# Attention units that alternate between two sets of PSUM banks, in a list-scheduled attention, mixing and FFN kernel

## The chip, the core and the metric

The kernel runs on one core of a Trainium2 chip. Its engines work side by side: TensorE (PE, and PEld for its weight loads) multiplies, VectorE (DVE) and ScalarE (ACT) work element by element, GpSimd (POOL) takes small element-wise work and some transfers, SyncE (SP) starts most transfers. Products land in PSUM, eight banks of 512 fp32 values on each of 128 partitions. The metric is the device time of one execution in microseconds (us).

## What is computed

Windowed attention over 8 batches and 8 heads, then a Fourier mixing over sequence and channels, a normalisation, and an FFN. Cut to what matters:

```python
# q, k, v: (8, 8, 576, 64); heads 0-3 look at 32 neighbours, heads 4-7 at 32 rows with stride 4
scores = np.where(masks, scale * q @ k.T, -1e9)
attn = exp(scores - max) / (sum + 1e-9);  x = attn @ v          # then (8, 576, 512)
mixed = np.real(np.fft.fft(np.fft.fft(x, axis=1), axis=2))
u = x + mixed
un = (u - mean) / sqrt(var + 1e-6)
out = u + np.maximum(un @ w_ch1, 0) @ w_ch2                     # 512 -> 2048 -> 512
```

## The kernel before

All work is written down as operations with an engine, an estimated cost, a priority and the buffers they use. A planner (class `Plan`) then runs a list schedule: whenever an engine is free in the plan, the ready operation with the lowest priority number that finds its buffers free is put next. The result is a fixed order of instructions on each engine. On the chip each engine follows its order and waits by semaphores.

Attention (`attend`) is cut into 96 units, 12 for each batch. A unit makes the scores of two blocks of 96 queries for two heads (4 products, L557), adds the mask and takes the negated maximum (4 DVE operations, L566), takes exponentials (4 ACT operations, L572), transposes (4 on PE, L585), copies the result to SBUF (ACT, L588), multiplies by the values (4 products, L592, called the AV products here) and divides by the sums (three DVE operations, L600, L603, L604). PE's profile rows show two matmuls for each product at L557 and L592.

Mixing of a batch (`mix`: products at L774, L796, L820, L826) follows its attention. Weights come in as 64-bit words and are narrowed on ACT and DVE (`narrow`). A fill (`fill`) runs the first 6 of 16 slices of the FFN for 256 tokens while attention of later batches goes on: up products at L954, down products at L970. After attention the rest of the FFN runs (L1223, L1311, L1278).

The eight PSUM banks are shared out by name: `pair` (banks 0 and 1) for scores, bank 2 for transposes (`pt`), bank 3 for AV products (`av`), banks 4 and 5 for mixing (`mixes`), banks 6 and 7 for the fills (`zs`). A ring of a tag hands its slots out in turn; `behind` says that a tag's first slot may be taken only when another tag's buffers are all done with. The scores of a unit use 256 columns of both banks of `pair`, one unit the lower half, the next the upper half. The AV products of each unit use bank 3.

Until the first fill takes its bank, the planner fills PE's free time with pairs of products on a blank tile (L503, called spins here; up to 250 pairs). They keep PE active and compute nothing that is used. They stand in PE's order like any other instruction.

The priority numbers (`P_...`) set the order of attention, mixing, weight loads, stores and fills against each other.

Of the kernel before, what the change touches and what calls it, by code (L numbers as in the profile page):

```python
# [36 lines left out]
NPE = 1  # L37
LO1 = 'DVE'
NFA = 5
P_QK0, P_V0 = -8.0, -7.0  # L40
P_ST, P_FD, P_WD, P_ST0, P_FD0, P_SPAN0, P_SPAN1 = -4.0, -12.0, -10.0, -14.0, -14.0, 4.0, 13.0
P_QK, P_V, P_TR, P_MIX, P_SPAN, P_W, P_WF, P_FILL, P_FILLT = -8.0, -7.0, -5.0, 2.0, 13.0, 24.0, 4.0, 45.0, 4.0
P_MIX0, P_MIX1 = -14.0, 0.0
T_SEQ, T_CHN = 20.0, 27.0
NCH = B * S // TOK
NREST = 4 * B
# [130 lines left out]
    __slots__ = ("eng", "cost", "fn", "prio", "bufs", "after", "waits", "ready", "start", "num", "nbytes")  # L177


PSUM_TAGS = ("sc", "half", "pt", "av", "mix", "ff", "duo0", "duo1", "duo2")  # L180


class Plan:
# [200 lines left out]
def fused_kernel(ctx: ExitStack, tc, q, k, v, w1, w2, seq, tail, chn, alt, mask, ident, perm, flip, out):  # L384
    nc = tc.nc
    plan = Plan()
# [21 lines left out]
    pair, pt_av, mixes, zs = [eight[i:i + 2] for i in range(0, 8, 2)]  # L408
    views = {"sc": pair, "pt": pt_av[:1], "av": pt_av[1:], "mix": mixes, "ff": zs}
    views.update({f"duo{i}": [lambda i=i: eight[2 * i:2 * i + 2]] for i in range(3)})  # L410
    plan.behind.update({"sc": ("half",), "duo0": ("sc", "half"), "duo1": ("pt", "av"), "duo2": ("mix",)})

    def halves():
        b = Buf(None, "half")
        plan.slots["half"] = 2
        line = plan.tags.setdefault("half", [])
        lo = 256 * (len(line) % 2)
        b.make = lambda: [t[:, lo:lo + 256] for t in pair]
        line.append(b)
        return b  # L420

    def ring(tag, of):
        b = Buf(None, tag)
        plan.slots[tag] = len(of)
        line = plan.tags.setdefault(tag, [])
        ap = of[len(line) % len(of)]
        b.make = ap if callable(ap) else lambda: ap
        line.append(b)
        return b

    def bank(tag):
        return ring(tag, views[tag])
# [53 lines left out]
    def start():  # L486
        dma(lambda: nc.sync.dma_start(out=mask_sb(), in_=mask), (), (mask_sb,), -7.9, QB * 3 * KB * 4)
        dma(lambda: nc.sync.dma_start(out=ident_sb(), in_=ident), (), (ident_sb,), -7.8, P * 3 * P * 4)
        dma(lambda: nc.sync.dma_start(out=perm_sb(), in_=perm), (), (perm_sb,), -7, QB * QB * 12)
        dma(lambda: nc.sync.dma_start(out=flip_sb(), in_=flip), (), (flip_sb,), 50, P * 32)  # L490

        def zero(t, eng, cost, fn, key=None, prio=-5.0):
            add(eng, cost, fn, (), ((t, key) if key is not None else t,), prio)

        zero(half, "DVE", 0.07, lambda: nc.vector.memset(half(), -0.5))
        for n, t in enumerate(kbs):
            zero(t, "DVE", 0.1, lambda t=t: nc.vector.memset(t()[:, 0:WIN], 0.0), "z", -6.0 + n)
        zero(blank, "DVE", 0.3, lambda: nc.vector.memset(blank().bitcast(F32), 0.0), None, -9.0)
        spin = Buf(ap=zs[0])
        for n in range(NSPIN):  # L500
            def turn_over():
                for _ in range(2):
                    nc.tensor.matmul(spin()[:, :2 * P], lhsT=blank()[:, :P], rhs=blank()[:, P:3 * P], start=True, stop=True)  # L503
            add("PE", 0.22, turn_over, (blank,), (spin,), SPIN, at=0.4 * n)
        for t in xs + xtail:
            zero(t, "DVE", 0.07, lambda t=t: nc.vector.memset(t()[:, C:C + 1], 0.0), "pad")
        def gaps():
            for r in (32, 96):
                nc.vector.memset(eot().bitcast(F32)[r:r + 32, 0], 0.0)
        zero(eot, "DVE", 0.4, gaps, ("gap", 0))  # L510
        zero(eot, "DVE", 0.2, lambda: nc.vector.memset(eot().bitcast(F32)[0:32, 1], 0.0), ("gap", 1))
        zero(ye, "DVE", 0.2, lambda: nc.vector.memset(ye().bitcast(F32), 0.0))
        for b in range(B):
            dma(lambda b=b: nc.sync.dma_start(
                out=xsm[b]()[0:1], in_=blank()[0:1].bitcast(F32),
            ), (blank,), ((xsm[b], "zero"),), 12 * b + 6, 2048)
        for i in range(2):
            for m in range(2):
                add("POOL", 0.06, lambda i=i, m=m: nc.gpsimd.dma_start(out=seq_sb[i]()[:, m], in_=seq[i, m]),
                    (), ((seq_sb[i], m),), 6 + i, P * 2 * NSP * 4, at=T_SEQ + i)  # L520
                add("POOL", 0.06, lambda i=i, m=m: nc.gpsimd.dma_start(out=chn_sb[i]()[:, m], in_=chn[i, m]),
                    (), ((chn_sb[i], m),), 9 + i, P * 2 * NEP * 4, at=T_CHN + i)
        add("POOL", 0.06, lambda: nc.gpsimd.dma_start(out=tail_sb(), in_=tail), (), (tail_sb,), 6.5, P * 3 * NSP * 4, at=T_SEQ + 0.5)
        add("POOL", 0.06, lambda: nc.gpsimd.dma_start(out=alt_sb(), in_=alt), (), (alt_sb,), 8, P * NEP * 4, at=T_SEQ + 4)
# [23 lines left out]
    def attend(b, dil, j, u, tq, kb, vt, xt, prio):  # L548
        blocks = (u, u + 3) if dil else (2 * u, 2 * u + 1)
        masks = DIL_MASK if dil else PLAIN_MASK  # L550
        sc = halves()

        def scores():
            for n, t in enumerate(blocks):
                for e in range(2):
                    ps = slice(64 * e, 64 * e + 64)
                    nc.tensor.matmul(  # L557
                        sc()[e][:QB, KB * n:KB * n + KB], lhsT=tq()[ps, QB * t:QB * t + QB],
                        rhs=kb()[ps, QB * t:QB * t + KB], start=True, stop=True,
                    )  # L560
        add("PE", 0.62, scores, (tq, kb), (sc,), prio)
        pm = attw("pm", [QB, 4, KB], F32, 3)
        mx = attw("mx", [QB, 4], F32, 3)
        for i in range(4):
            def masked(i=i):
                nc.vector.tensor_tensor_reduce(  # L566
                    pm()[:, i], sc()[i % 2][:QB, KB * (i // 2):KB * (i // 2) + KB], mask_sb()[:, masks[blocks[i // 2]]],
                    -0.125, 3.0e38, ALU.add, ALU.min, mx()[:, i:i + 1],
                )
            add("DVE", 0.21, masked, (sc, mask_sb), ((pm, i), (mx, i)), prio)  # L570
        for i in range(4):
            add("ACT", 0.295, lambda i=i: nc.scalar.activation(  # L572
                out=pm()[:, i], in_=pm()[:, i], func=AF.Exp, bias=mx()[:, i:i + 1], scale=-1.0),
                ((mx, i),), ((pm, i),), prio)
        ps = bank("pt")
        for i in range(4):
            def turn(i=i):
                t = blocks[i // 2]
                if dil:
                    order = perm_sb()[:, t % 3]  # L580
                elif t < 3:
                    order = ident_sb()[:QB, 0, :QB]
                else:
                    order = ident_sb()[:QB, 1, P - QB:]
                nc.tensor.transpose(ps()[:, QB * i:QB * i + QB], pm()[:, i], order)  # L585
            add("PE", 0.087, turn, ((pm, i), perm_sb, ident_sb), ((ps, i),), prio)
        pt = attw("ptsb", [P, 4, QB], F32, 3)
        add("ACT", act(4 * QB) - 0.05, lambda: nc.scalar.copy(  # L588
            out=pt().rearrange("p i q -> p (i q)"), in_=ps()[:, :4 * QB]), (ps,), (pt,), prio)
        av = bank("av")  # L590
        for i in range(4):
            add("PE", 0.173, lambda i=i: nc.tensor.matmul(  # L592
                av()[:QB, 65 * i:65 * i + 65], lhsT=pt()[:, i],
                rhs=vt()[:, i % 2, blocks[i // 2]], start=True, stop=True),
                (pt, vt), ((av, i),), prio)
        sums, rinv = attw("sums", [QB, 4], F32, 3), attw("rinv", [QB, 4], F32, 3)

        def view():
            return av()[:QB, :260].rearrange("p (t h d) -> p t h d", t=2, h=2)
        add("DVE", 0.075, lambda: nc.vector.tensor_scalar(  # L600
            sums(), av()[:QB, :260].rearrange("p (i d) -> p i d", d=65)[:, :, D], 1e-9, None, op0=ALU.add),
            (av,), (sums,), prio)
        add("DVE", 0.1, lambda: nc.vector.reciprocal(out=rinv(), in_=sums()), (sums,), (rinv,), prio)  # L603
        add("DVE", dve(256), lambda: nc.vector.tensor_tensor(  # L604
            out=xt()[:, :, j::2, :], in0=view()[:, :, :, 0:D],
            in1=rinv().rearrange("p (t h) -> p t h", t=2).unsqueeze(3).broadcast_to([QB, 2, 2, D]), op=ALU.mult),
            (av, rinv), ((xt, j),), prio)
        if j == 1:
            store(b, dil, u, xt, prio)
# [792 lines left out]
```

## Time and profile before

| | |
|---|---|
| median of 3 runs | 1089.67 us (1085.24 to 1094.61) |
| the profiled execution's own time | 1086.16 us |
| its span in the trace | 1084.4 us |
| PE busy | 1067.1 us (98%) |
| DVE busy | 775.9 us (72%) |
| ACT busy | 517.7 us (48%) |
| spins on PE | 248 matmuls, all in the first 108 us |

The span runs from the first to the last instruction of the program; 1.76 us of the execution's time lie outside it. Ends of matmuls are modelled, so PE's busy time covers small stalls between matmuls. A matmul's cost in a row of them is read from start to start, which the chain of waits gives.

### The profile page before, as it was taken

The numbers are of one execution on the slowest core, as the hardware profiler recorded it, in microseconds if no ns is written. First come the engines' busy times: TensorE is split into PE (matmuls) and PEld (weight loads), VectorE is DVE, ScalarE is ACT, GpSimd is POOL, SyncE is SP. The second block draws the span as 40 slices with busy tenths as digits, with TensorE's granted clock in tenths as the row PEclk, the third lists the DMA queues.
The fourth block names the chain that finished last, engine by engine and source line by source line (L and its number), as shares of the span: only waits on it lengthen the run. The fifth ranks groups of instructions, "written<-read, shape, count | busy, mean of one in ns | idle before, by whom it ended". The sixth has DMA issues, their size and how long they took to land.

```text
span 1084.4 us, 21164 instructions
## 1 busy us (share of the span) xinstructions
PE 1067.1 (98%) x7683; PEld 958.8 (88%) x7683; DVE 775.9 (72%) x2384; ACT 517.7 (48%) x1282; POOL 280.7 (26%) x328
## 2 busy tenths in 40 slices
PE   7999999999999999999999999999999999999998
PEld 6888888898889888889989898999898999888987
DVE  4889988777677757976774657676766767676746
ACT  5777656547456553434342543434342525252532
POOL 2236463644343326553321110101010101010200
PEclk9999999999999999999999999999999999999999
DMA  9686566745464326254443402223233332333221
GB/s 342 223 269 196 165 167 180 235 134 176 121 210 140 115 64 176 78 163 127 148 137 98 117 20 59 98 60 98 60 104 74 96 81 88 88 82 91 67 71 39
DMA packets 103800, 137.10 MB, mean 126 GB/s; under 512 B 9144, under 2 KB 61816, under 8 KB 103696
## 3 DMA queue, kind: packets, MB, share of 16 engines
q1 hardware_dynamic: 100128, 126.85, 39.9%
q0 software_dynamic: 3040, 8.09, 2.5%
q8 instruction: 60, 0.98, 0.4%
q10 hardware_dynamic: 528, 0.82, 0.2%
q14 instruction: 44, 0.36, 0.1%
HBM read 97.92 MB, written 37.80 MB: 125 GB/s over the span
## 4 chain that ended last, share of the span: by engine, by line
PE 89%; DVE 5%; DMA 3%; issue 1%; ACT 1%; POOL 0%; SPq 0%; DVEq 0%; ACTq 0%
PE bank L1223 23%; PE bank L1311 19%; PE bank L970 12%; PE bank L954 12%; PE bank L592 5%; PE bank L557 5%; PE bank L820 3%; PE bank L585 3%; PE bank L774 2%; PE bank L503 2%; PE bank L1278 1%; DMA ut<-in_w_dram 1%; DMA vt<-in_v_dram 1%; DVE pm L566 1%; DMA wst<-in_w_dram 1%
## 5 line engine op out<-in xcount | busy, mean ns | idle before, releaser
L1223 PE MATMUL bank<-low,wb 128*128 128x512 f32 x1080 | 260.4, 393 | 0.0
L1223 PEld LDWEIGHTS bank<-low,wb 128*128 128x128 f32 x1080 | 198.4, 188 | 41.0
L954 PE MATMUL bank<-ut,low 128*128 128x256 f32 x1296 | 175.3, 286 | 1.2 <-DVE low L962 0.8
L954 PEld LDWEIGHTS bank<-ut,low 128*128 128x128 f32 x1296 | 160.9, 189 | 5.2 <-DVE low L962 1.9
L572 ACT ACTIVATE pm<-pm,mx 96x128 f32<-96x128 f32 x384 | 131.2, 394 | 53.8 <-DVE mx L566 49.6
L970 PE MATMUL bank<-low 128*128 128x512 f32 x648 | 155.2, 392 | 0.9 <-DVE low L962 0.9
L998 POOL DMA_INDIRECT ut<-us,flip_sb x20 | 40.3, 2014 | 406.9 <-DVE ut L1055 249.5
L970 PEld LDWEIGHTS bank<-low 128*128 128x128 f32 x648 | 119.1, 188 | 24.7 <-DVE low L962 1.1
L1229 ACT ACTIVATE xa<-bank 128x256 f32<-128x256 f32 x90 | 34.4, 382 | 180.0 <-PE bank L1223 180.0
L566 DVE CUSTOM_DVE_ANT_0 pm<-bank,mask_sb 96x128 f32<-96x128 f32 x384 | 93.0, 278 | 34.5 <-PE bank L557 31.6
L1250 DVE TENSOR_TENSOR y<-xa 128x384 f32<-128x384 f32 x45 | 25.1, 557 | 106.6 <-ACT xa L1229 106.3
L592 PE MATMUL bank<-vt,ptsb 128*96 128x65 f32 x768 | 82.2, 247 | 3.0 <-DVE xt L604 2.5
L592 PEld LDWEIGHTS bank<-vt,ptsb 128*96 128x96 f32 x768 | 76.4, 164 | 9.3 <-DVE xt L604 5.3
L1077 DVE STREAM_TRANSPOSE ut<-ut 128x512 f32<-128x512 f32 (+1 forms) x76 | 71.5, 983 | 18.1 <-DMA ut<-us 17.1
L962 DVE SCALAR_TENSOR_TENSOR low<-bank,low 128x256 fp32r<-128x256 f32 x108 | 45.2, 419 | 47.8 <-ACT low L960 47.1
L960 ACT ACTIVATE low<-bank 128x256 fp32r<-128x256 f32 x108 | 41.3, 382 | 78.1 <-PE bank L954 78.0
L1311 PEld LDWEIGHTS bank<-w2s,low 128*128 128x128 f32 x588 | 73.8, 190 | 2.4
L1044 DVE TENSOR_TENSOR ut<-ut,bank 128x512 f32<-128x512 f32 (+1 forms) x136 | 73.1, 547 | 2.3
L1311 PE MATMUL bank<-w2s,low 128*128 128x256 f32 x588 | 74.4, 281 | 0.0
L557 PE MATMUL bank<-kb,tq 64*96 64x128 f32 x768 | 63.2, 285 | 4.4 <-DVE mx L566 2.3
L1311 PEld LDWEIGHTS bank<-w2s,hm 128*128 128x128 f32 x483 | 59.7, 189 | 1.9
L1311 PE MATMUL bank<-w2s,hm 128*128 128x256 f32 x483 | 60.2, 280 | 0.0
(147 smaller groups left out, 1808.3 us busy)
## 6 DMA issues: line engine op xcount, KB each, us to landing
vt<-in_v_dram SPq DMA_DIRECT2D x32, 390.0 KB
us<-uc SPq DMA_DIRECT2D x36, 257.0 KB
tq<-in_q_dram SPq DMA_DIRECT2D x32, 288.0 KB
part<-row SPq DMA_DIRECT2D x36, 256.0 KB
wst<-in_w_dram SPq DMA_DIRECT2D x18, 512.0 KB
ut<-us SPq DMA_DIRECT2D x36, 256.0 KB
ut<-part SPq DMA_DIRECT2D x36, 256.0 KB
kb<-in_k_dram SPq DMA_DIRECT2D x31, 288.0 KB
```

The costliest lines, as they stand in the source:

```text
L557: nc.tensor.matmul(sc()[e][:QB, KB * n:KB * n + KB], lhsT=tq()[ps, QB * t:QB * t + QB], rhs=kb()[ps, QB * t:QB * t + KB], start=True, stop ...
L566: nc.vector.tensor_tensor_reduce(pm()[:, i], sc()[i % 2][:QB, KB * (i // 2):KB * (i // 2) + KB], mask_sb()[:, masks[blocks[i // 2]]], -0.1 ...
L572: add("ACT", 0.295, lambda i=i: nc.scalar.activation(out=pm()[:, i], in_=pm()[:, i], func=AF.Exp, bias=mx()[:, i:i + 1], scale=-1.0), ((mx ...
L592: add("PE", 0.173, lambda i=i: nc.tensor.matmul(av()[:QB, 65 * i:65 * i + 65], lhsT=pt()[:, i], rhs=vt()[:, i % 2, blocks[i // 2]], start= ...
L954: nc.tensor.matmul(z()[:, :n_tok], lhsT=wf()[:, a, kk], rhs=ut()[:, p, kk], start=(kk == 0 and n == 0), stop=(kk == KT - 1 and n == 2),)
L960: add("ACT", act(n_tok) - 0.05, lambda: nc.scalar.activation(out=h()[:, 0, :n_tok], in_=z()[:, :n_tok], func=AF.Relu), (z,), ((h, 0),), prio)
L962: add("DVE", dve(n_tok), lambda: nc.vector.scalar_tensor_tensor(h()[:, 1, :n_tok], z()[:, :n_tok], 0.0, h()[:, 0, :n_tok].bitcast(F32), op ...
L970: nc.tensor.matmul(acc(), lhsT=h()[:, a, P * s:P * s + P], rhs=wf()[:, p], start=(first and n == 0), stop=(last and n == 2),)
L1044: add("DVE", dve(C if at in (outer, inner) else TOK1), lambda: nc.vector.tensor_tensor(out=blocks(part())[:, at], in0=blocks(part())[:, at ...
L1077: nc.vector.transpose(out=o[back], in_=x[:, g])
L1223: nc.tensor.matmul(z(), lhsT=wb1[NF1 + 2 * p + f]()[:, a, kk], rhs=ut()[:, x, kk], start=(kk == 0 and n == 0), stop=(kk == KT - 1 and n == 2),
L1311: nc.tensor.matmul(acc()[block // 2][:, TOK1 * (block % 2):TOK1 * (block % 2) + TOK1], lhsT=hl()[:, a, i], rhs=w2s[p]()[:, j, x], start=(o ...
```

## The change

Scores of the first 20 units get a ring of two bank sets, the lower halves of banks 0 and 1 and those of banks 4 and 5, which belong to mixing. AV products of the first 29 units alternate between bank 3 and bank 6, which belongs to the fills. Mixing may take its banks only after the 20 units, a fill only after the 29. The spins move from bank 6 to bank 7. Twelve priority numbers are changed (the diff shows one line of them).

```diff
+NSC2, NAV2 = 20, 29
 P_QK0, P_V0 = -8.0, -7.0
-P_ST, P_FD, P_WD, P_ST0, P_FD0, P_SPAN0, P_SPAN1 = -4.0, -12.0, -10.0, -14.0, -14.0, 4.0, 13.0
+P_ST, P_FD, P_WD, P_ST0, P_FD0, P_SPAN0, P_SPAN1 = -5.1, -11.2, -10.0, -19.4, -13.9, 7.8, 13.0
...
-PSUM_TAGS = ("sc", "half", "pt", "av", "mix", "ff", "duo0", "duo1", "duo2")
+PSUM_TAGS = ("sc", "half", "half2", "av2", "pt", "av", "mix", "ff", "duo0", "duo1", "duo2")
...
     views.update({f"duo{i}": [lambda i=i: eight[2 * i:2 * i + 2]] for i in range(3)})
+    views["av2"] = [pt_av[1], zs[0]]
+    plan.behind.update({"av": ("av2",), "ff": ("av2",), "half": ("half2",), "mix": ("half2",)})
     plan.behind.update({"sc": ("half",), "duo0": ("sc", "half"), "duo1": ("pt", "av"), "duo2": ("mix",)})
 
-    def halves():
+    def halves(n):
+        if n < NSC2:
+            return ring("half2", [lambda: [t[:, 0:256] for t in pair], lambda: [t[:, 0:256] for t in mixes]])
         b = Buf(None, "half")
...
-        spin = Buf(ap=zs[0])
+        spin = Buf(ap=zs[1])
...
-        sc = halves()
+        sc = halves(12 * b + 6 * dil + 3 * j + u)
...
-        av = bank("av")
+        av = bank("av2" if 12 * b + 6 * dil + 3 * j + u < NAV2 else "av")
```

In the lists below bankN is PSUM bank N; a line of the changed kernel is 5 higher than the same line before. "waits" names the engine or queue that a row's semaphores belong to.

DVE, the masks of the second unit of the first batch (`pm_247` is its tile of masked scores), before:

```order
L566 ISA pm_247,mx_248<-bank0_135,mask_sb_145 96x128
L566 ISA mx_248 96x1
L566 ISA pm_247,mx_248<-bank1_136,mask_sb_145 96x128
L566 ISA mx_248 96x1
L566 ISA pm_247,mx_248<-bank0_135,mask_sb_145 96x128 [waits PE_49]
```

And now:

```order
L571 ISA pm_247,mx_248<-bank4_139,mask_sb_145 96x128 [waits PE_49]
L571 ISA mx_248 96x1
L571 ISA pm_247,mx_248<-bank5_140,mask_sb_145 96x128 [waits PE_49]
L571 ISA mx_248 96x1
L571 ISA pm_247,mx_248<-bank4_139,mask_sb_145 96x128
```

Before, the second unit's masks waited for PE a second time in the middle of the unit, for scores of the third unit, which PE had been given for the same two banks; now they wait once, for their own scores in banks 4 and 5.

PE, a little later in the first batch, from a spin on: the AV products (`ptsb`), transposes (`pm`) and scores (`kb2`) of three neighbouring units, before:

```order
L503 MATMUL bank6_141<-blank_160 128x256 x2
L585 MATMUL bank2_137<-ident_sb_146,pm_335 128x96 [waits Activation_49]
L592 MATMUL bank3_138<-vt_208,ptsb_401 96x65 [waits DMAHW0_49,DVE_49]
L592 MATMUL bank3_138<-vt_208,ptsb_401 96x65 x3
L585 MATMUL bank2_137<-ident_sb_146,pm_335 128x96 x3
L557 MATMUL bank0_135<-kb2_159,tq_225 96x128 [waits DVE_49]
L557 MATMUL bank1_136<-kb2_159,tq_225 96x128 [waits DVE_49]
```

And now:

```order
L508 MATMUL bank7_142<-blank_160 128x256 x2
L597 MATMUL bank6_141<-vt_208,ptsb_402 96x65 [waits DMAHW0_49,Activation_49]
L597 MATMUL bank6_141<-vt_208,ptsb_402 96x65 x3
L590 MATMUL bank2_137<-ident_sb_146,pm_336 128x96 x4
L562 MATMUL bank0_135<-kb2_159,tq_225 96x128 [waits DVE_49]
L562 MATMUL bank1_136<-kb2_159,tq_225 96x128 [waits DVE_49]
```

The AV products went to bank 6 and no longer wait for DVE, which has the division of the unit ahead to do in bank 3, and they stand ahead of all four transposes.

PE, the stretch ahead of the first fill, with spins between the units' products, before:

```order
L503 MATMUL bank6_141<-blank_160 128x256 x4
L585 MATMUL bank2_137<-ident_sb_146,pm_1505 128x96 [waits Activation_49]
L585 MATMUL bank2_137<-ident_sb_146,pm_1505 128x96 x3
L503 MATMUL bank6_141<-blank_160 128x256 x20
L592 MATMUL bank3_138<-vt_1149,ptsb_1492 96x65 [waits DVE_49]
L592 MATMUL bank3_138<-vt_1149,ptsb_1492 96x65 x3
L557 MATMUL bank0_135<-kb2_159,tq_1281 96x128 [waits DMAHW4_49,DMAHW3_49]
```

And now:

```order
L508 MATMUL bank7_142<-blank_160 128x256 x8
L597 MATMUL bank3_138<-vt_1304,ptsb_1852 96x65 [waits DVE_49]
L597 MATMUL bank3_138<-vt_1304,ptsb_1852 96x65 x3
L508 MATMUL bank7_142<-blank_160 128x256 x8
L590 MATMUL bank2_137<-ident_sb_146,pm_1948 128x96 [waits Activation_49]
L590 MATMUL bank2_137<-ident_sb_146,pm_1948 128x96 x3
L508 MATMUL bank7_142<-blank_160 128x256 x14
L597 MATMUL bank3_138<-vt_1528,ptsb_1931 96x65 [waits DMAHW7_49,DVE_49]
```

Counted over PE's whole order, the first fill stood behind the AV products of 28 units and 248 spins, and now stands behind those of 37 units and 240 spins. Ahead of the AV products of unit 13 there were 122 spins and now are 76; between those of units 29 and 37 there were none and now are 88.

## Rows read from the trace of the kernel before

**Rows 1.** The page's head: busy time, share of the span, instructions.

```profile
span 1084.4 us, 21164 instructions
...
PE 1067.1 (98%) x7683; PEld 958.8 (88%) x7683; DVE 775.9 (72%) x2384; ACT 517.7 (48%) x1282; POOL 280.7 (26%) x328
```

**Rows 2.** Stretches: length, busy time and (instructions) by engine, granted PE clock, DMA.

```profile
8.00:30.00 22.00, 17.32 (x176) 14.31 (x176) 12.97 (x95) 15.39 (x46) 0.54 (x1) 1.00 1.10 386
30.00:78.00 48.00, 47.74 (x470) 43.36 (x468) 40.46 (x206) 36.12 (x99) 14.64 (x14) 1.00 0.72 227
78.00:110.00 32.00, 31.24 (x295) 28.58 (x294) 29.60 (x132) 23.30 (x63) 19.63 (x27) 1.00 0.66 208
...
440.00:1080.00 640.00, 639.62 (x4013) 576.42 (x4010) 438.76 (x819) 257.26 (x568) 97.80 (x76) 1.00 0.32 89
```

**Rows 3.** The spins: durations in ns, first and last start in us.

```profile
L503 PE MATMUL bank<-blank x248: 274/283/579, 1.4 to 108.0; 128*128 128x256 f32 x124
```

**Rows 4.** PE in order of time, to the first fill: start, us, idle before.

```profile
6.87 1.12 PE L557 MATMUL bank<-kb,tq 64*96 64x128 f32 x16
...
16.58 0.68 PE L557 MATMUL bank<-kb,tq 64*96 64x128 f32 x8 [0.57 <-DVE mx L566]
...
24.04 0.89 PE L592 MATMUL bank<-vt,ptsb 128*96 128x65 f32 x8 [0.31 <-DVE xt L604]
...
108.42 2.02 PE L954 MATMUL bank<-ut,low 128*128 128x256 f32 x15
```

**Rows 5.** The chain of waits, pieces in order of time: start, us, what.

```profile
46.34 1.46 PE bank L503 x12
47.80 0.65 PE bank L592 x8
...
48.74 0.61 PE bank L557 x8
...
52.99 0.33 PE bank L585 x4
...
85.49 0.95 PE bank L774 x7
...
89.38 1.45 PE bank L820 x12
```

**Rows 6.** DVE in order of time, one unit's operations: start, us, idle before.

```profile
19.18 0.28 DVE L566 CUSTOM_DVE_ANT_0 pm<-bank,mask_sb 96x128 f32<-96x128 f32 x1
...
19.39 0.28 DVE L566 CUSTOM_DVE_ANT_0 pm<-bank,mask_sb 96x128 f32<-96x128 f32 x1
...
19.82 0.15 DVE L600 TENSOR_SCALAR sums<-bank 96x4 f32<-96x4 f32 x1
20.00 0.17 DVE L603 RECIPROCAL rinv<-sums 96x4 f32<-96x4 f32 x1
20.77 0.29 DVE L566 CUSTOM_DVE_ANT_0 pm<-bank,mask_sb 96x128 f32<-96x128 f32 x1 [0.59 <-PE bank L557]
...
20.98 0.42 DVE L604 TENSOR_TENSOR xt<-bank,rinv 96x256 f32<-96x256 f32 x1
21.32 0.28 DVE L566 CUSTOM_DVE_ANT_0 pm<-bank,mask_sb 96x128 f32<-96x128 f32 x1
```

**Rows 7.** PE's waits (weight loads), 0 to 80 us: us in total, times, longest.

```profile
PEld bank L592 <- DVE xt L604: 1.6, 4, 0.5
...
PEld bank L557 <- DVE xt L604: 1.3, 1, 1.3
PEld bank L557 <- DVE mx L566: 1.3, 3, 0.8
```

**Rows 8.** PE's waits (matmuls) for a transfer, 0 to 80 us.

```profile
PE bank L557 <- DMA tq<-in_q_dram: 2.0, 2, 1.1
```

**Rows 9.** PE's waits (weight loads), 80 to 412 us.

```profile
PEld bank L592 <- DVE xt L604: 3.7, 9, 0.8
PEld bank L557 <- DVE mx L566: 3.4, 9, 0.6
```

More of the change, by code (lines that the diff above doesn't have):

```diff
@@ L39 @@
 NFA = 5
+NSC2, NAV2 = 20, 29
 P_QK0, P_V0 = -8.0, -7.0
-P_ST, P_FD, P_WD, P_ST0, P_FD0, P_SPAN0, P_SPAN1 = -4.0, -12.0, -10.0, -14.0, -14.0, 4.0, 13.0
-P_QK, P_V, P_TR, P_MIX, P_SPAN, P_W, P_WF, P_FILL, P_FILLT = -8.0, -7.0, -5.0, 2.0, 13.0, 24.0, 4.0, 45.0, 4.0
-P_MIX0, P_MIX1 = -14.0, 0.0
+P_ST, P_FD, P_WD, P_ST0, P_FD0, P_SPAN0, P_SPAN1 = -5.1, -11.2, -10.0, -19.4, -13.9, 7.8, 13.0
+P_QK, P_V, P_TR, P_MIX, P_SPAN, P_W, P_WF, P_FILL, P_FILLT = -8.0, -7.7, -5.0, 1.9, 13.0, 24.0, 3.9, 50.3, 4.3
+P_MIX0, P_MIX1 = -16.0, 2.5
 T_SEQ, T_CHN = 20.0, 27.0
```

## The prediction, made before the changed kernel ran

> **What bounds the kernel now.** I read the page's head first. PE is busy for 98% of the span, so little is left between its instructions [rows 1]. The stretches say where that little is: from 440 us to 1080 us PE is busy 639.62 of 640 us, and nothing that happens to attention can shorten it [rows 2]. The end of the program is therefore set by PE's sum of work plus whatever PE loses earlier. It loses in two forms. One is the spins: 248 matmuls without use, the last at 108.0 us [rows 3]. They stand in PE's order and are run whether or not anyone is late. The other is waiting, seen as idle time ahead of scores and AV products [rows 4].
>
> The loss up to the first fill can be added up, because the pieces of the chain of waits give the cost of each kind of product from start to start [rows 5]: a unit's scores 0.61 us, its transposes 0.33, its AV products 0.65, a spin 1.46/12 = 0.122, a mixing product 0.95/7 = 0.136 (L774) or 1.45/12 = 0.121 (the others, and the transposes of normalised rows). By PE's order there stand ahead of the first fill the scores of 35 units (21.4 us), transposes of 32 (10.6), AV products of 28 (18.2), 30 products at L774 and 45 others of mixing (4.1 and 5.4) and 8 more transposes (1.0): 60.6 us in all. Twenty-four spins come before the first score at 6.87 us [rows 4], the other 224 make 27.3 us. The first fill starts at 108.42 us [rows 4], which is 101.55 us after the first score. So 101.55 - 60.6 - 27.3 = 13.7 us were waits and restarts after waits.
>
> What PE waits for there is the unit's own chain. Scores wait for masks of the unit ahead, AV products for the division of the unit ahead [rows 4, 7]; DVE in turn waits 0.59 us for scores in the middle of its run of units [rows 6]. DVE is 59% busy from 8 to 30 us, 84% from 30 to 78 and 92% from 78 to 110 [rows 2].
>
> **Spins.** There are 8 fewer, 8 x 0.122 = **-1.0 us**. This is the only gain that is certain from the order. The 46 spins that go from ahead of unit 13 are not gained: most come back between units 29 and 37, where PE may not start a fill that used to cover it.
>
> **The longer way to the first fill.** By the new order there stand ahead of it the scores of 42 units (25.6 us), transposes of 40 (13.2), AV products of 37 (24.1), the same mixing (9.5) and 16 transposes (1.9): 74.3 us, 13.7 us more than before. It is work that PE would do later anyway, so it costs nothing. With equal waits the first fill would start at 108.42 + 13.7 - 1.0 = 121.1 us. The fills that are pushed back (405 instead of 483 up products ahead of unit 93) move behind attention, where PE has no gaps [rows 2].
>
> **Waits in the first 80 us.** Three of them are what a second set of banks takes away: AV products for the division 1.6 us, scores for the division 1.3, scores for masks 1.3, together 4.2 us [rows 7]. The next thing late is a transfer: scores wait 2.0 us for queries [rows 8], and units that come sooner reach it sooner. Bounds: all 4.2 us go, or nothing goes because every one turns into that wait. I take **-3.5 us**, nearer the first, since only two of the waits before were transfers.
>
> **Waits from 80 us to the first fill.** Units 21 to 29 still have two AV banks. From 80 to 412 us the two kinds of wait are 3.7 and 3.4 us for some 75 units [rows 9], so eight units carry 7.1 x 8/75 = **-0.8 us**. Bounds 0 and 1.5.
>
> **The priorities.** They reorder stores, weight loads and mixing through the rest of attention; no row prices that. The nearest row is the same 7.1 us [rows 9]: it could lose all of it or, at the other end, add as much. With 59 units behind the first fill instead of 68, I take **-1.0 us**, and keep both ends.
>
> **Lent banks.** Mixing has its first product after the scores of 26 units before and of 27 now, past the 20 that hold its banks, so that gate costs 0. If it held mixing longer, a wait would stand in PE's order ahead of L774; none is added. The longest cover for the fills' bank is the spins between units 29 and 37, 88 x 0.122 = 10.7 us, already counted.
>
> **The sum**: -1.0 - 3.5 - 0.8 - 1.0 = -6.3 us on a span of 1084.4, so 1078.1, and 1079.9 for the execution beside 1086.16. The median of the runs stands 3.5 us above the profiled one, so it becomes 1089.67 - 6.3 = **1083.4 us**, 0.6% less.
>
> **Rival 1: DVE becomes what PE waits for, and it is slower.** The new order asks DVE for nine more units ahead of the first fill. A unit costs it 4 x 0.21 + 0.15 + 0.17 + 0.34 = 1.5 us from start to start [rows 6], nine 13.5; one more block of weights less one fill's work I set at 1.5 (estimate, 0 to 3). DVE was busy 83.0 us from 8 to 110 us [rows 2], so about 81.5 to the first fill, 81% of the time. It now has 96.5 us to do. My sum puts the first fill at 121.1 - 4.3 = 116.8 us and so needs DVE at 96.5/108.8 = 89%. At the old 81% the first fill comes at 8 + 119 = 127 us, 6 us of new waits, and the whole is 6 - 1.0 = 5 us **slower: 1094.7 us**. The change is worth nothing at 96.5/114.1 = 85%, and slower by over 1% below 77%. For it speaks that DVE was only 84% busy from 30 to 78 us; against it, that it waited for PE there, which the new banks undo, and that it reached 92% from 78 to 110 us.
>
> **Rival 2: the chain loosens more.** At that 92%, held from 8 us on, DVE would be through at 8 + 105 = 113 us. The waits then shrink by 8 us instead of 4.3, and with spins and later waits the gain is 10 to 11 us: **1079 us**, 1% faster. Against it: the first 30 us move data at 386 GB/s with the queues full [rows 2], which no bank helps.
>
> **Rival 3: the clock.** In all stretches the granted clock was 1.00, the 2.4 GHz level, even from 8 to 30 us where PE idled 4.7 of 22 us [rows 2]. If fewer spins between units 9 and 13 let it fall to 1.2 GHz for those 10 us, products would take twice as long there, some 8 us more: **1091 us**. The Trainium skill ("TensorE: Matmul & The Clock Gate", section "A second HAM failure mode: psum-queue depth-cycling") speaks against a change like this: it tells of a kernel that cycled through PSUM banks and whose small gaps made the clock go up and down. By that rule the sum would turn into this rival; the trace, with larger gaps at 1.00, does not bear it out.
>
> **Chances.** My forecast, 1080.5 to 1088: 0.52. Rival 2 and beyond, 1072 to 1080.5: 0.24. No gain to rival 1, 1088 to 1096: 0.18. Rival 3 or a worse order of the rest: 0.06. The range reaches from 1074 into rival 1, 1094. A measurement of this kernel tells about 1% (11 us) from no change. Faster than 1078.8 is most of rival 2, 0.20; slower than 1100.6 is 0.05; the rest, 0.75, within 1%.
>
> **What would show it.** In the profile after: 240 spins; the first up product of a fill between 114 and 119 us (127 for rival 1, 113 for rival 2); DVE at 89% from 8 us to there; no AV products that wait for the division before unit 29, and fewer mask operations that wait for scores; a clock of 1.00 throughout. I would be wrong if PE's idle time grew between 110 and 440 us, where the new priorities act and I have no price, or if PE lost time behind attention, where more fills now stand.

## The result, and the profile of the changed kernel

The changed kernel takes **1077.51 us** (median of 4 runs, 1077.06 to 1077.87); the kernel before, in runs on the same chip, 1087.88 us (4 runs, 1085.24 to 1094.61). The ratio is 0.9895, with a 95% interval of 0.9848 to 0.9943: about 1% faster. The forecast was 1083.4 us with a range of 1074 to 1094. The profiled executions are 1077.06 us against 1086.16, their spans 1075.3 us against 1084.4: 9.1 us to account for.

The medians differ by 1.3 us more than that, because the kernel before loses clock in about half of its runs: in 31 of 64 later runs of it, on four chips, the records give a mean granted clock of 0.983 to 0.994 and 1088.7 to 1097.3 us, in the other 33 a clock of 0.999 or 1.000 and 1084.2 to 1086.8 us (two of the four runs above lie in the longer group by their times), while all four runs of the changed kernel stand at 0.999 or 1.000.

The page's head of the changed kernel (busy time, share, instructions):

```profile
span 1075.3 us, 21155 instructions
...
PE 1062.8 (99%) x7675; PEld 957.3 (89%) x7675; DVE 770.8 (72%) x2384; ACT 515.5 (48%) x1282; POOL 278.0 (26%) x328
```

Its stretches; the last of these rows reaches to the first fill:

```profile
8.00:30.00 22.00, 19.82 (x214) 17.35 (x214) 16.52 (x113) 18.49 (x56) 0.00 (x0) 1.00 1.03 365
30.00:78.00 48.00, 48.00 (x489) 43.38 (x489) 42.28 (x236) 39.83 (x115) 19.15 (x22) 1.00 0.86 281
78.00:110.00 32.00, 31.66 (x309) 28.55 (x307) 29.22 (x150) 22.50 (x62) 19.25 (x24) 1.00 0.76 241
8.00:118.00 110.00, 107.48 (x1082) 97.02 (x1083) 95.79 (x519) 85.00 (x241) 41.52 (x49) 1.00 0.85 277
```

Against [rows 2] PE, DVE and ACT are all busier from 8 to 30 us (PE 19.82 us instead of 17.32, DVE 16.52 instead of 12.97): the units follow closer on each other. DVE is 95.79/110 = 87% busy up to the first fill. The clock is 1.00 in each.

PE in order of time, up to the first fill:

```profile
13.67 1.12 PE L562 MATMUL bank<-kb,tq 64*96 64x128 f32 x16 [1.47 <-DMA tq<-in_q_dram]
14.72 0.89 PE L597 MATMUL bank<-vt,ptsb 128*96 128x65 f32 x8
...
24.28 0.89 PE L597 MATMUL bank<-vt,ptsb 128*96 128x65 f32 x8 [0.71 <-ACT ptsb L593]
...
118.08 0.60 PE L959 MATMUL bank<-ut,low 128*128 128x256 f32 x3
```

The waits for masks and divisions of [rows 4] are gone from the start of this stretch, where a transfer of queries and a copy by ACT end last instead; up to the first fill one wait for masks is left, 0.34 us at 100.18 us. The first fill starts at 118.08 us instead of 108.42. PE's waits (weight loads) from 0 to 80 us:

```profile
PEld bank L562 <- DVE xt L609: 1.6, 1, 1.6
...
PEld bank L597 <- ACT ptsb L593: 0.9, 1, 0.9
...
PEld bank L562 <- DVE mx L571: 0.2, 1, 0.2
```

There is no AV product left that waits for a division (1.6 us in [rows 7]); scores that wait for masks went from 1.3 to 0.2 us, and the one wait of scores for a division went from 1.3 to 1.6. The same from 80 to 412 us, where [rows 9] had 3.7 and 3.4:

```profile
PEld bank L562 <- DVE mx L571: 3.0, 7, 0.8
...
PEld bank L597 <- DVE xt L609: 1.2, 3, 0.7
```

On the other side DVE waited for PE. Its waits in the changed kernel from 8 to 118 us:

```profile
DVE pm L571 <- PE bank L562: 5.6, 8, 1.7
DVE sums L605 <- PE bank L597: 4.0, 10, 1.3
```

and in the kernel before from 8 to 108.4 us:

```profile
DVE pm L566 <- PE bank L557: 15.7, 16, 5.0
DVE sums L600 <- PE bank L592: 3.8, 6, 1.2
```

Masks waited 15.7 us for scores, and now 5.6. That this is the direct work of the second set of score banks is shown by e11 below.

**Where the 9.1 us came from.** From the starts of all matmuls one gets PE's loss in a stage: its length, less a fixed price for each matmul in it, a start-to-start time as it is usual in rows of them without waits (a spin 0.118 us, a product of scores 0.153, of AV 0.170, a transpose 0.081, an up product 0.116, a down product 0.226, and so on). The rest is waiting, slower starts behind a wait and, where the clock falls, slower matmuls.

| stage, loss in us | before | changed | difference |
|---|---|---|---|
| spins (248 and 240; work, not loss) | 29.3 | 28.3 | -0.9 |
| first score to first fill | 13.92 | 10.59 | -3.3 |
| to the last AV product | 22.17 | 19.71 | -2.5 |
| to the last mixing product | 4.01 | 1.52 | -2.5 |
| to the end (FFN) | 12.61 | 12.74 | +0.1 |

The pieces add up to -9.1. More than half of the gain lies behind the first fill. The prices are a choice: with the median start-to-start times in their place the differences of the stages move by up to 0.4 us, their sum does not, and the level of the losses, above all that of the FFN, moves more.

### The profile page after: what moved, and what is told of

Same layout as the page of the kernel before. It is cut to its first block, busy times and chain, and to the rows that moved or that the text cites. A ratio compares the mean times of both kernels' runs of the same rounds, so it can differ in the third digit from the quotient of the medians.

```text
span 1075.3 us, 21155 instructions
## 1 busy us (share of the span) xinstructions
PE 1062.8 (99%) x7675; PEld 957.3 (89%) x7675; DVE 770.8 (72%) x2384; ACT 515.5 (48%) x1282; POOL 278.0 (26%) x328
## 4 chain that ended last, share of the span: by engine, by line
PE 93%; DVE 2%; DMA 2%; ACT 1%; issue 0%; POOL 0%; POOLq 0%; ACTq 0%; DVEq 0%
PE bank L1228 23%; PE bank L1316 20%; PE bank L959 14%; PE bank L975 13%; PE bank L597 5%; PE bank L562 5%; PE bank L825 3%; PE bank L779 3%; PE bank L590 3%; PE bank L508 3%; PE bank L1283 1%; DMA vt<-in_v_dram 1%; DVE pm L571 1%; DMA ut<-in_w_dram 1%; ACT pm L577 1%; PE bank L801 1%
## 5 line engine op out<-in xcount | busy, mean ns | idle before, releaser
L959 PE MATMUL bank<-ut,low 128*128 128x256 f32 x1296 | 170.8, 285 | 0.1
L959 PEld LDWEIGHTS bank<-ut,low 128*128 128x128 f32 x1296 | 160.4, 189 | 3.2 <-DVE low L967 0.5
L593 ACT COPY ptsb<-bank 128x384 f32<-128x384 f32 x96 | 45.3, 472 | 35.8 <-PE bank L590 28.2
```

The costliest lines, as they stand in the source:

```text
L593: add("ACT", act(4 * QB) - 0.05, lambda: nc.scalar.copy(out=pt().rearrange("p i q -> p (i q)"), in_=ps()[:, :4 * QB]), (ps,), (pt,), prio)
L959: nc.tensor.matmul(z()[:, :n_tok], lhsT=wf()[:, a, kk], rhs=ut()[:, p, kk], start=(kk == 0 and n == 0), stop=(kk == KT - 1 and n == 2),)
```

## The experiments

Three theories were set against each other. **B**: the lent banks alone bring the gain. **P**: the new numbers alone bring it. **S**: both are needed, because together they let the planner write an order with fewer spins. The results stand in one table, with the losses as above in us (the ratio is against the kernel before on the same chip):

| kernel | median (range), us | ratio (95%) | span | spins | first fill at | loss to it | to last AV | to last mixing | rest |
|---|---|---|---|---|---|---|---|---|---|
| before (profiled) | | | 1084.4 | 248 | 108.4 | 13.9 | 22.2 | 4.0 | 12.6 |
| changed | 1077.5 (1077.1 to 1077.9) | 0.9895 (0.985, 0.994) | 1075.3 | 240 | 118.1 | 10.6 | 19.7 | 1.5 | 12.7 |
| e1_old_banks | 1105.3 (1100.9 to 1110.5) | 1.0147 (1.009, 1.021) | 1099.1 | 302 | 107.8 | 12.8 | 26.2 | 5.4 | 16.7 |
| e2_old_prio | 1088.3 (1087.3 to 1089.1) | 0.9971 (0.994, 1.000) | 1086.3 | 302 | 128.4 | 12.7 | 19.3 | 4.3 | 12.7 |
| e3_scores_only | 1092.5 (1090.4 to 1097.9) | 1.0056 (1.003, 1.009) | 1091.2 | 296 | 118.6 | 17.9 | 22.7 | 1.5 | 12.8 |
| e4_av_only | 1096.2 (1095.4 to 1100.8) | 1.0108 (1.008, 1.014) | 1093.6 | 290 | 142.4 | 15.1 | 19.9 | 4.4 | 18.5 |
| e5_no_spins | 1088.1 (1084.8 to 1104.1) | 1.0009 (0.997, 1.005) | 1092.1 | 24 | 134.5 | 52.8 | 20.1 | 1.5 | 12.8 |
| e7_first_old | 1076.4 (1076.2 to 1076.7) | 0.9912 (0.989, 0.993) | 1074.4 | 240 | 118.1 | 10.6 | 18.8 | 1.5 | 12.8 |
| e8_step_back | 1085.4 (1085.0 to 1087.9) | 0.9966 (0.994, 0.999) | 1083.2 | 302 | 128.5 | 12.6 | 18.9 | 1.5 | 12.7 |
| e9_banks_and_step | 1081.0 (1079.3 to 1082.8) | 0.9917 (0.988, 0.995) | 1079.7 | 240 | 118.7 | 11.8 | 20.2 | 5.0 | 12.6 |
| e10_half_spins | 1076.7 (1073.8 to 1081.2) | 0.9912 (0.988, 0.995) | 1072.0 | 132 | 115.1 | 21.3 | 19.4 | 1.5 | 12.8 |
| e11_same_banks | 1079.5 (1078.5 to 1087.5) | 0.9920 (0.989, 0.995) | 1078.1 | 240 | 120.4 | 12.8 | 20.2 | 1.5 | 12.8 |
| e12_late_half | 1073.9 (1073.3 to 1075.4) | 0.9877 (0.985, 0.990) | 1071.9 | 150 | 115.2 | 18.9 | 19.2 | 1.5 | 12.7 |
| e13_early_half | 1077.9 (1077.0 to 1083.0) | 0.9916 (0.989, 0.994) | 1077.2 | 222 | 119.6 | 14.2 | 19.4 | 1.5 | 13.5 |

The first score comes at 5.8 to 6.9 us in these traces, behind the same 24 spins, so a difference of less than 1 us between two spans says little by itself. All edits are made to the changed kernel, e9 excepted. Spins compute nothing that is used, so none of these kernels leaves out a part of the reference.

**e1_old_banks: the new numbers without the banks.**

```diff
-NSC2, NAV2 = 20, 29
+NSC2, NAV2 = 0, 0
```

> The new priority numbers with no bank lent. PE's order then holds 302 spins instead of 240 and the first fill stands behind 24 units. Theory S (time follows the spins that stand in PE's order, 0.122 us each, plus the waits of a single bank set): 1077.5 + 62 x 0.122 = 1085.1, plus up to 6 us of waits that come back, 1085 to 1091. Theory P (the priorities carry the gain, since most of it lies behind the first fill): at or below 1080.

Measured: 1105.3 us, 1.5% slower than before. Theory P falls. S has the direction right and the size wrong. The order has 302 spins, 62 x 0.118 = 7.3 us more than the changed kernel, and PE loses more in every stage too, 4 us of it in the FFN. One wait there is the longest of the stretch from 430 to 615 us:

```profile
PE bank L959 <- DVE r L668: 3.1, 1, 3.1
PE bank L975 <- DVE low L967: 1.7, 1, 1.7
```

**e2_old_prio: the banks with the old numbers.** All three lines of numbers are put back, of which one is shown:

```diff
...
-P_MIX0, P_MIX1 = -16.0, 2.5
+P_MIX0, P_MIX1 = -14.0, 0.0
```

> The banks are lent, all priority numbers as before. PE's order holds 302 spins. Theory S: 1077.5 + 7.6 = 1085 us, as slow as the kernel before, though the AV products and the masks wait less. Theory B (the banks carry the gain, spins stand where PE would wait anyway): 1078 to 1081.

Measured: 1088.3 us, at best 0.6% below before. Theory B falls; S is nearer, 3 us too low. The banks alone do lower the losses (12.7 and 19.3 us for 13.9 and 22.2), but the order holds 302 spins and comes to its first fill only at 128.4 us: 54 x 0.118 = 6.4 us of spins against 4 us of gain.

**e8_step_back: one of the twelve numbers put back.** `P_WF` is the step in priority from one slice of the FFN's weights to the next.

```diff
-P_QK, P_V, P_TR, P_MIX, P_SPAN, P_W, P_WF, P_FILL, P_FILLT = -8.0, -7.7, -5.0, 1.9, 13.0, 24.0, 3.9, 50.3, 4.3
+P_QK, P_V, P_TR, P_MIX, P_SPAN, P_W, P_WF, P_FILL, P_FILLT = -8.0, -7.7, -5.0, 1.9, 13.0, 24.0, 4.0, 50.3, 4.3
```

> The changed kernel with one number put back: the step between the priorities of the weight blocks, 3.9 to 4.0. PE's order then holds 302 spins instead of 240. Theory S: 1085 us, nearly all of the gain gone by one tenth in one number. Theory B: no change, 1077 to 1079.

Measured: 1085.4 us, 7.9 above the changed kernel. In the spans the difference is also 7.9 us: 302 spins for 240 are 7.3 and the loss to the first fill 2.0, less 0.8 to the last AV product and 0.5 ahead of the first score. With a step of 3.9 in place of 4.0 the weights of the sixth slice get a number that is 0.5 lower, and the planner's first fill, behind which no spin may stand, comes 62 spins earlier. S's 1085 us holds.

**e9_banks_and_step: the kernel before with the banks and this one number.** The diff is against the kernel before.

```diff
+NSC2, NAV2 = 20, 29
...
-P_QK, P_V, P_TR, P_MIX, P_SPAN, P_W, P_WF, P_FILL, P_FILLT = -8.0, -7.0, -5.0, 2.0, 13.0, 24.0, 4.0, 45.0, 4.0
+P_QK, P_V, P_TR, P_MIX, P_SPAN, P_W, P_WF, P_FILL, P_FILLT = -8.0, -7.0, -5.0, 2.0, 13.0, 24.0, 3.9, 45.0, 4.0
```

> The kernel before with the banks lent and one number changed, the step of the weight blocks (4.0 to 3.9). PE's order holds 240 spins, as in the changed kernel. Theory S: 1077.5, with the waits behind the first fill as they come; if the other eleven numbers carry the 5 us that were gained behind the first fill, 1082.

Measured: 1081.0 us, near the second of the two. It has the changed kernel's 240 spins and its first fill 0.6 us later, and then loses 5.0 us where the changed kernel loses 1.5, between the last AV product and the last mixing product. PE's waits there, in e9:

```profile
PE bank L959 <- DVE low L967: 1.6, 2, 1.0
PE bank L975 <- DVE low L967: 0.9, 1, 0.9
```

in the kernel before:

```profile
PE bank L970 <- DVE low L962: 0.9, 1, 0.9
PE bank L954 <- DVE low L962: 0.6, 1, 0.6
```

and in the changed kernel, in the whole stage:

```profile
PE bank L825 <- DVE sq L841: 0.3, 1, 0.3
```

Fills that wait for DVE to narrow their weights (`low`), 2.5 of these 3.5 us, are what the other numbers remove. They also leave less in the stage, 267 matmuls in place of 390; the rest of the fills' work moves behind it.

**e7_first_old: the numbers of the first two batches put back**, those of the later batches kept.

```diff
-P_ST, P_FD, P_WD, P_ST0, P_FD0, P_SPAN0, P_SPAN1 = -5.1, -11.2, -10.0, -19.4, -13.9, 7.8, 13.0
+P_ST, P_FD, P_WD, P_ST0, P_FD0, P_SPAN0, P_SPAN1 = -5.1, -11.2, -10.0, -14.0, -14.0, 4.0, 13.0
...
-P_MIX0, P_MIX1 = -16.0, 2.5
+P_MIX0, P_MIX1 = -14.0, 0.0
```

> The changed kernel with the five numbers of the first two batches put back (stores, mixing loads and mixing of batch 0, mixing of batch 1). PE's order holds 240 spins still. If the numbers of all later batches carry the 2.5 us gained between the last attention unit and the last mixing product: 1077.5 to 1078.5. If those of the first two batches carry it: 1080 to 1081, as with all eleven numbers put back (1081.0).

Measured: 1076.4 us, 1 us below the changed kernel and with its loss of 1.5 us ahead of the last mixing product. With e9 the spans go 1084.4, 1079.7, 1074.4, 1075.3: banks and step -4.7 us, the six numbers of the later batches and of the fills -5.3, the first batches' +0.9. The last is small, but the runs of the two kernels do not overlap (1076.2 to 1076.7 us and 1077.1 to 1077.9). Which of the six numbers matter was not tried.

**e3_scores_only and e4_av_only: one set of banks at a time.**

```diff
-NSC2, NAV2 = 20, 29
+NSC2, NAV2 = 20, 0
```

> The changed kernel with the second bank set for scores alone; all AV products use bank 3. PE's order holds 296 spins, the first fill stands behind 28 units. Theory S (time follows the spins in PE's order at 0.122 us each, and the waits): 1077.5 + 6.8 = 1084.3 and some 2 to 4 us of waits for the division, 1086 to 1089. Theory of separate gains (each bank set carries half of the early gain): 1079 to 1080.

```diff
-NSC2, NAV2 = 20, 29
+NSC2, NAV2 = 0, 29
```

> The changed kernel with the second bank for AV products alone; scores use the two halves of banks 0 and 1. PE's order holds 290 spins, the first fill stands behind 40 units. Theory S: 1077.5 + 6.1 = 1083.6 and up to 2.5 us of waits of scores for masks, 1084 to 1086. Theory of separate gains: 1079 to 1080.

Measured: 1092.5 and 1096.2 us, both slower than before, and slower than S had it by 4 and 10 us. That each set has a gain of its own falls under these numbers: either alone leaves an order of 290 or 296 spins. The numbers were those found for both sets; one set with numbers of its own was not tried. e3 also lost clock (below). e4 loses 6 us more than the changed kernel in the FFN, where it has the same single 3.1 us wait of L959 for DVE's `r` as e1. Why these two orders come to that wait was not tried.

**e11_same_banks: the two sets of scores as halves of the same banks**, in an order of instructions that is the changed kernel's on every engine.

```diff
-            return ring("half2", [lambda: [t[:, 0:256] for t in pair], lambda: [t[:, 0:256] for t in mixes]])
+            return ring("half2", [lambda: [t[:, 0:256] for t in pair], lambda: [t[:, 256:512] for t in pair]])
```

> The changed kernel with the same order on every engine and the same gates, but the second set for scores is the upper half of banks 0 and 1 instead of banks 4 and 5. If sharing a bank is what makes masks wait for later scores and scores for later masks: masks wait for scores 5 to 10 us more up to the first fill, the first fill comes 2 to 4 us later, and the time is 1079 to 1082. If the pacing comes from the order alone: 1077 to 1078.

Measured: 1079.5 us, 2.0 above the changed kernel; span 1078.1, 2.8 us above; first fill at 120.4 us. DVE's waits from 8 to 121 us:

```profile
DVE pm L571 <- PE bank L562: 15.1, 17, 5.3
DVE sums L605 <- PE bank L597: 2.4, 5, 0.9
```

The masks' waits are back at 15.1 us. The order being the same, this is the price of sharing: PE's next scores and DVE's masks of the unit ahead wait for each other in one bank, though they use different columns. The waits are semaphores of the program; on the masks of the first six units they stand at the same places as in the kernel before. Of these 9.5 us, 2.8 come through to the span.

**e5, e10, e12, e13: what the spins do.** Four kernels thin them out and keep the rest of the order: none behind the first 24 (e5), one in place of two behind the first 24 (e10), one in place of two from the 61st on (e12), and one in place of two from the 25th to the 60th (e13). e12 has e7's numbers besides.

```diff
-            add("PE", 0.22, turn_over, (blank,), (spin,), SPIN, at=0.4 * n)
+            add("PE", 0.22, turn_over if n < 12 else lambda: None, (blank,), (spin,), SPIN, at=0.4 * n)
```

> The changed kernel in the same order, with no spins behind the first 24 (216 matmuls whose results are not used are left out). Theory S taken to the end: 216 x 0.122 = 26 us less, 1051. Theory D (DVE, busy most of the time from 8 us to the first fill, then is what PE waits for): at most 14 us less, 1064 to 1075. Theory C (the spins hold the clock): the granted clock falls to the 1.2 GHz level in the first 118 us and the time is at or above 1077.

```diff
-                for _ in range(2):
+                for _ in range(2 if n < 12 else 1):
```

> The changed kernel in the same order with one spin where there were two, behind the first 24 (132 spins in all instead of 240; the 108 left out have no used result). If the spins' time is lost time as long as the clock holds: 1077.5 - 108 x 0.122 = 1064. If they stand where PE would wait anyway: 1075 to 1077.5, with the waits to the first fill up by as much as the spins go down. If PE's clock falls as it did with no spins: above 1078, with a mean granted clock below 0.99.

```diff
-                for _ in range(2):
+                for _ in range(2 if n < 30 else 1):
```

> The changed kernel with the five numbers of the first two batches put back (1076.35 by itself) and one spin where there were two from the 31st spin operation on, some 30 us into the span (150 spins in all). If the early spins hold the clock and the later ones can be halved, with most of their time coming back as waits: 1071 to 1074, with granted clocks of 0.998 to 1.000 in all runs. If the late ones matter for the clock too: above 1076, with clocks below 0.995.

```diff
-                for _ in range(2):
+                for _ in range(1 if 12 <= n < 30 else 2):
```

> The changed kernel with one spin where there were two in 18 spin operations alone, from the first score to some 30 us (222 spins in all, 18 x 0.122 = 2.2 us less). If the early spins hold the clock: runs with granted clocks of 0.99 to 0.996 beside runs at 0.998 and above, as with all spins halved, and a median of 1077 to 1082. If they only cost time: 1075.3 to 1077, clocks 0.998 and above.

Measured: 1088.1, 1076.7, 1073.9 and 1077.9 us. In e5's span 216 spins, 25.5 us, are gone, and the loss to the first fill is 42.2 us larger; of its three theories C is the one that fits. Stretches of e5:

```profile
10.00:20.00 10.00, 7.43 (x59) 6.56 (x59) 4.24 (x32) 5.48 (x18) 0.00 (x0) 0.66 1.09 393
...
50.00:60.00 10.00, 7.67 (x51) 6.00 (x48) 6.93 (x34) 6.95 (x20) 2.00 (x1) 0.50 0.55 187
```

From 50 to 60 us the granted clock was 0.50, the 1.2 GHz level, with no spins between the units; the changed kernel has 1.00 in the same stretches. The rest of the order being the same, this shows that spins hold the clock here. In e10, 108 spins less took 12.7 us out, and 10.7 us came back, at most 1.7 us of it by the slower clock of the first row below (an estimate from its 0.83 over 10 us). e12's traced run shows the same at a clock of 1.00, with 10.6 us out and 8.3 back: the spins stand mostly where PE would wait anyway. The same stretch of e10, then of e12, then of e13:

```profile
10.00:20.00 10.00, 7.67 (x76) 6.91 (x76) 4.70 (x35) 5.62 (x17) 0.00 (x0) 0.83 1.09 392
```

```profile
10.00:20.00 10.00, 8.10 (x94) 7.03 (x93) 5.62 (x43) 7.02 (x23) 0.00 (x0) 1.00 1.09 392
```

```profile
10.00:20.00 10.00, 8.14 (x67) 7.03 (x66) 4.97 (x38) 6.46 (x21) 0.00 (x0) 0.72 1.09 392
```

With eighteen early spins less the clock fell from 10 to 20 us in e13's traced run (0.72), and with 90 later ones less it held in e12's (1.00). Not every run does so: three of e13's six stand at a mean clock of 0.998 or 0.999, and two of e12's five at 0.996, where all were expected at 0.998 or more. Nor does the count of spins decide alone, for e3 has 296 and lost clock in this place (last section). e10's runs spread over 7 us and e12's over 2. **e12 is the fastest kernel of the study**: 1073.9 us, ratio 0.9877 (0.985 to 0.990), 3.6 us below the changed kernel, of which e7's numbers are about 1. Its span is 2.5 us below e7's, 0.6 of it by an earlier first score.

## Why the prediction was right, and which terms were off

The direction was right, and the time lies in the range, but that range was 20 us wide, and the size was not right: 9.1 us of span for 6.3. The measured 1077.5 us lies outside the prediction's own 1080.5 to 1088 (chance 0.52), in the band that it gave to rival 2 (0.24), and rival 2 is not how it came there.

- **Spins.** Forecast -1.0, measured -0.9 us. The count was right, but the term is not as free-standing as it was put: the order's count of spins says how long the plan expects PE to be free, and what is taken out by hand comes back for the most part as waits (e10, e12). What the change spares is 62 spins against the order that its banks have with a step of 4.0 (e8). How much of e8's 7.9 us is the spins themselves, and how much the later first fill that they stand for, is not shown: no run took spins out of that order.
- **The longer way to the first fill.** Forecast 13.7 us of work moved ahead of the fill at no cost. The fill came 9.7 us later with 3.3 us less of loss and 0.9 us less of spins ahead of it, so it is 13.9, and the loss in the FFN changed by 0.1 us. Right.
- **Waits to the first fill.** Forecast -3.5 and -0.8, together -4.3, first fill 116.8 us (114 to 119); measured -3.3 and 118.1. The mechanism is the one stated, and its size 1 us less. Of the 4.2 us of [rows 7] 1.8 are left, for the wait of scores for a division did not go; the DMA's 2.0 us [rows 8] became the 1.5 us shown above, with a new one of 0.7 us for ACT. Another wait for ACT, of the transposes, went without having been priced; it stood in the list of [rows 7]:

```profile
PEld bank L585 <- ACT ptsb L588: 1.7, 2, 1.5
```

  The Trainium skill's page "PSUM — Partial Sum Buffer", section "PSUM bank collisions raise a hardware error", asks that two engines be kept apart by bank (or bank and quadrant of partitions) and not by address. e11 puts a price on keeping apart by bank here, where the columns were free and the bank was not: 2.8 us of span, 2.0 of the medians.
- **Rival 1, DVE as the bound.** It needed DVE at 89% and had its break-even at 85%; DVE reached 87%, because the masks' waits fell from 15.7 to 5.6 us. It did not come about.
- **Rival 2** asked for the first fill at 113 us. It came at 118, so its mechanism is not what brought the time near its 1079 us; that the time is near is chance.
- **Rival 3, the clock.** It stayed at 1.00 in the traced run. So what the Trainium skill tells of cycling through PSUM banks ("TensorE: Matmul & The Clock Gate", section "A second HAM failure mode: psum-queue depth-cycling") did not come about here. The runs went the other way: with both sets and all spins (changed, e2, e7, e8, e9, e11) 44 of 45 show a mean clock of 0.997 or more, with one set or none (before, e1, e3, e4) 40 of 78 show less. So the second sets go with a steadier clock; why is not shown. The rival's premise, that fewer spins let the clock fall, did hold in e5, e10 and e13.
- **Lent banks.** Forecast 0. PE's loss behind the first fill shrank, so no cost shows; it was not measured by itself.
- **The priorities: the term that was mis-sized.** Forecast -1.0 us with bounds of 7.1 on either side, "no row prices that"; measured -5.0 behind the first fill, in equal halves before and after the last AV product. Not all of it is theirs: e9, with the banks and the step alone, has 2.0 us of the first half already (20.2 for 22.2) and nothing of the second (5.0 for 4.0), so 3.9 us of the 5.0 go with the other eleven numbers. The second half came with the other numbers, and e7 shows with which: those of the later batches and of the fills, with which no fill waits for its narrowed weights between the last AV product and the last mixing product. The nearest row was sought among the waits of attention units [rows 9]. PE's waits for `low` between the last AV product and the last mixing product, 0.9 and 0.6 us as shown above, would have been the nearer one. The stage's whole loss was 4.0 us. And the numbers did more than this term held: with the banks lent, all twelve are worth 11.0 us of span (e2 to the changed kernel, 1086.3 to 1075.3), most of it by the spins ahead of the first fill, which the prediction took from the new order as they were.
- **The median.** The sum for the span was 1078.1 us and the span 1075.3, 2.8 off. The other 3 us of the miss of 5.9 come from the step that kept the median 3.5 us above the profiled run: it was 0.45 above it. That offset was before's loss of clock in half its runs: two of the three runs behind that median, 1089.67 and 1094.61 us, belong to that half by their times. Among runs at full clock the change is worth 8 to 9 us, 0.8%; the rest of the measured 1% is clock.

So the runs bear out S, refined: banks and step together give the order with 240 spins and shorter waits (-4.7 us), the numbers of the later batches and of the fills go with -5.3, in good part waits for narrowed weights, and the first batches' numbers give 0.9 back. Open are what the step alone does in the kernel before (e1 has it without the banks, but with the other eleven numbers), why e1 and e4 come to a 3.1 us wait in the FFN, and where the kernel before loses its clock in half its runs, since its trace is of a run at 1.00.

## What to carry to other kernels

In this list-scheduled kernel lending banks paid only together with numbers that let the plan use it: one set alone, or the banks with the old numbers, left orders that were slower or no faster, so buffers and priorities should be searched together and filler counted in the order. Filler on PE costs little where PE would wait anyway, and is to be kept where the clock would fall; each piece is to be tried by itself. When an offset between the profiled run and the median is carried into a forecast, look first at the runs' clocks.

## What was not expected of the hardware

- The granted clock stood at 0.50 for a whole stretch in which PE was recorded busy for 7.67 of 10 us (e5, 50 to 60 us), and in e3 for one where it was recorded busy throughout, with 62 matmuls in place of the changed kernel's 100; it had fallen in the stretch before, where PE was recorded busy for 8.06 of 10 us. Stretches of e3:

```profile
10.00:20.00 10.00, 8.06 (x67) 6.90 (x67) 4.25 (x32) 5.86 (x19) 0.00 (x0) 0.74 1.14 382
20.00:30.00 10.00, 10.00 (x62) 8.49 (x62) 5.25 (x34) 5.43 (x16) 0.00 (x0) 0.50 1.05 385
```

- PE's busy time can hide a slower start: the same eight AV matmuls take 0.89 us at 14.72 us in the changed kernel and 0.81 us at 52.05 us, and no idle time is recorded ahead of either. PE in order of time there:

```profile
50.75 1.46 PE L508 MATMUL bank<-blank 128*128 128x256 f32 x10
52.05 0.81 PE L597 MATMUL bank<-vt,ptsb 128*96 128x65 f32 x8
```

- Two halves of one PSUM bank did not serve as two buffers: with the same order, 15.1 us of DVE's waits against 5.6 (e11). These waits are the program's semaphores; what the chip would do without them no run here shows.
